# One planned list for attention and the feed-forward layers: the pairs m = 8 to 13 move into the second half of the first two chunks

## The chip, the cores and the metric

The kernel runs on one core of one Trainium2 chip. The metric is device time in microseconds (us). The core's engines are TensorE (PE in the profile; PEld is its weight loading), VectorE (DVE), ScalarE (ACT), GpSimd (POOL) and SyncE (SP). SP, ACT and POOL also issue DMAs. Each engine works through its own list of instructions in order; semaphores tie the lists together.

## What is computed

Banded attention of 8 batches, 8 heads, 576 positions and 64 features, and on its output a two-layer feed-forward network with a leaky ReLU. Cut to what matters:

```python
batch, n_heads, seq, head_dim = (8, 8, 576, 64)
n_tokens, d_model, d_ff = (4608, 512, 2048)
...
scores = scale * np.matmul(q, k.transpose(0, 1, 3, 2))
mask = (rel >= 0) & (rel < window)          # window = 64
scores = np.where(mask, scores, -1000000000.0)
scores = scores - np.max(scores, axis=-1, keepdims=True)
attn = np.exp(scores)
attn = attn / (np.sum(attn, axis=-1, keepdims=True) + 1e-09)
attn_out = np.matmul(attn, v)
...
x = attn_out.transpose(0, 2, 1, 3).reshape(B * S, H * D)
h = x @ w_in
g = np.maximum(0.01 * h, h)
return (g @ w_out)
```

## The kernel before, in words

**Tiling.** The 4608 tokens are 9 chunks of 512 (`CH`). A block of 64 queries of one batch is a unit; there are 72 units (`NU`), eight to a chunk, and attention handles them in pairs, m = 0 to 35, four pairs to a chunk. The hidden width of 2048 is 16 slices f of 128 (`FT`; `half` is 8). Numbers are kept as a high and a low part (`F32R` tiles; hi and lo, wh and wl, gh and gl), and each product is three matmuls: high by high, high by low, low by high.

**Weights.** They arrive as 64-bit floats, 32 tiles n (`fetch_w`, L200, through three buffers `raw`). Each passes `bits` (L215), `sign` (L219), `abs` (L223, on ACT), `clamp` (L227), `join` (L232), `chi` (L235, on ACT) and `rest` (L241). Even n are slices of w_in, odd n of w_out.

**The feed-forward layers.** Chunks 0 to 2 go by jobs (c, f): `mm1` (12 matmuls, L508), then on ACT the leaky ReLU and the high part, on DVE the low part, then `mm2` (12 matmuls, L554) one job later. Chunks 3 to 8 go in three product stages of two chunks each (`s` = 0, 1, 2): the first layer as 7 block products instead of 8 for each of 8 slices (L1103, 336 matmuls), the second as plain matmuls (L1128, 384). These stages read prepared weights from HBM (`w_first`, `w_second`) through a ring of four tiles that POOL fills (L1090).

**Who sets the order.** Up to the 19 jobs of `JOBS` the order is written out by hand in `ORDER`, before its bar. Then a loop over 16 jobs (chunks 0 and 1, f = 8 to 15; L641 to L674) weaves five steps of `late`, the part of `ORDER` after the bar, into each job (`PACE`), and from the sixth job on the attention of m = 8 to 11 (`scores_2`, `shield_2`, `second_2`, `sums_2`, `values_2`, `invert_2`, `norm_2`). From the eighth job on it also spreads over the jobs the 40 stores of weights to HBM (`kept`, L632: 24 to `w_first`, 16 to `w_second`). Everything after that loop is entered into a plan with `op`: an engine, an estimated duration, what it comes after, a rank. `arrange` then simulates five engines, always takes the ready operation of the lowest rank, and so writes each engine's list. A load counts 0.08 us on SP and about 2.2 us until it lands; the matmuls of attention count as ready 0.5 us after their inputs.

**One pair m in the plan** (`attend`, `normalise`): `scores_of` (PE, L268, into the PSUM banks s and t); `shield_of` (DVE, L781: scale and mask into an SBUF tile, two halves j); `all_of` with max (POOL, L787, a reduction over the partitions whose result stands on all of them); `minus_of` (DVE, L791); `exp_of` (ACT, L795). For m < 20 (`early`) the sums are matmuls with ones (`add_of`, L808) copied out by ACT (`sums_of`, L815); for later m they are two more reductions on POOL. Then `compact_of` or `compact_early` (SP DMA, L822, L819) brings the sums to a 128 x 8 tile, `inverse_of` (DVE, L826, L827) inverts it, `rows_of` (SP, L830) stores it to HBM, `spread_of` (SP, two DMAs, L840) reads it back spread over partitions, `values_of` (PE, L849) multiplies by v, `take_of` (ACT, L856, early only) copies that out of PSUM, `product_of` (DVE, L860) scales it, `keep_of` (SP, two DMAs with runs of 64 numbers, L864) stores it to `x_rows`. There are two buffers of each kind, taken by m % 2.

m = 8 to 11 take no such trip: POOL's sums stand on all partitions (L440), the reciprocal is taken there 512 wide (L467), and `norm_2` writes chunk 2's x tiles directly.

**Between attention and products.** `x_build` reads x_rows back (SP, L928), forms the sums of blocks the seven products need (DVE, L936) and splits them (ACT L952, DVE L955). `prepared` does the same for w_in: fetch from `w_single` (ACT queue, L1042), joins (DVE, L1045), high (ACT, L1048), low (DVE, L1051), four stores to `w_first` (ACT queue, L1055). Both have to wait for buffers that chunk 2's jobs (`early_first`, L977; `early_second`, L984; leaky ReLU L1005, high L1008, low L1011) set free.

Of the kernel before, what the change touches and what calls it, by code (L numbers as in the profile page):

```python
# [24 lines left out]
P = 128  # L25
# [12 lines left out]
PAIRED = 12  # L38
PACE = 5
KEPT = 7  # L40
# [56 lines left out]
def band_attention_ffn(ctx: ExitStack, tc: tile.TileContext, qT, kB, vW, vL, w_in, w_out, eye_mask, out, outT):  # L97
# [43 lines left out]
    def k_of(m):  # L141
        if m >= PAIRED:
            return (ks[0], later.get("k"), ks[1])[(m - PAIRED) % 3]
# [42 lines left out]
    w_first = dram.tile([half * 7 // 4, P, 4, 512], F32, name="w_first")  # L186
    w_second = dram.tile([half, P, 2, 1024], F32, name="w_second")

    def first_at(f, k):
        n = 7 * f + k  # L190
        return w_first[n // 4, :, n % 4].rearrange("p (i c) -> p i c", i=2)
# [203 lines left out]
    def scores_2(u):  # L395
        if u >= NU:
            return
        ps = [bank(next(t), f"s{u}_{j}") for j, t in enumerate((of_a, of_h))]
        quarter_scores(u // 2, ps, False)
        probs[u] = ps  # L400
        load_k(u // 2 + 1)
        load_q(u // 2 + 2)

    def shield_2(u):

        if u >= NU:
            return
        ps = probs.pop(u)
        a = mask_of(u).bitcast(F32)
        n = a.shape[1]  # L410
        a = flat(a)[:, None, :].broadcast_to([P, H // n, n * QB])
        for j in range(2):
            e, s = (x.rearrange("a (b c) -> a b c", c=n * QB) for x in (probs_of[:, j], ps[j]))
            nc.vector.scalar_tensor_tensor(e, s, SCALE, a, ALU.mult, ALU.add)
            if j == 0:
                first_most = most(u, j)
        exps_2(0, first_most)
        probs[u] = most(u, 1)

    def most(u, j):  # L420
        mx = temps[:, 512:]
        nc.gpsimd.partition_all_reduce(mx, probs_of[:, j], P, ReduceOp.max)
        return mx

    def exps_2(j, mx):
        e = probs_of[:, j]
        nc.vector.tensor_tensor(e, e, mx, ALU.subtract)
        nc.scalar.activation(e, e, AF.Exp)

    def second_2(u):  # L430

        if u < NU:
            exps_2(1, probs.pop(u))

    def sums_2(u):
        if u >= NU:
            return
        raw = flat(wk.tile([P, 512, 2], U32, tag="raw", bufs=3, name=f"n{u}")).bitcast(F32)
        for j in range(2):
            nc.gpsimd.partition_all_reduce(raw[:, 512 * j : 512 * j + 512], probs_of[:, j], P, ReduceOp.add)  # L440
        probs[u] = raw

    def values_2(u):
        if u >= NU:
            return
        raw = probs.pop(u)
        v = [v_heads(u // 2, w) for w in range(2)]
        ps = bank(next(of_a), f"o{u}")
        for w in range(2):
            for p in range(NP):  # L450
                for j in range(2):
                    c = (2 * p + w) * QB
                    nc.tensor.matmul(
                        ps[64 * j : 64 * j + 64, c : c + QB], v[w][:, 2 * p + j, :D], probs_of[:, j, c : c + QB],
                        start=True, stop=True,
                    )
        probs[u, 0] = ps, raw
        load_v(u // 2 + 1)

    def invert_2(u):  # L460
        if u >= NU:
            return
        ps, raw = probs[u, 0]
        r, t = raw[:, :512], raw[:, 512:]
        nc.vector.tensor_scalar_add(r[:64], r[:64], 1e-9)
        nc.vector.tensor_scalar_add(r[64:], t[64:], 1e-9)
        nc.vector.reciprocal(r, r)  # L467

    def norm_2(u):
        if u >= NU:  # L470
            return
        ps, raw = probs.pop((u, 0))
        r, t = raw[:, :512], raw[:, 512:]
        nc.vector.tensor_tensor(t, ps, r, ALU.mult)
        hi, lo = x_of(u)
        t = t.rearrange("a (b c) -> a b c", b=NP)
        nc.scalar.copy(hi, t)
        return partial(nc.vector.tensor_tensor, lo, t, hi.bitcast(F32), ALU.subtract)

    later = {}

    def open_room():

        e, n, v = (wk.tile([P, 512, 2], U32, tag="raw", bufs=3, name=f"late_{x}") for x in "env")
        e, n, v = (flat(x).bitcast(F32).rearrange("p (a b) -> p a b", a=2) for x in (e, n, v))
        k = flat(wk.tile([P, NP, 2, D], F32, tag="y", bufs=1, name="late_k").rearrange("p a b c -> p a (b c)"))
        o = [wk.tile([P, 512], F32, tag="o", name=f"late_o{i}") for i in range(2)]
        later.update(e=e, n=n, v=v, k=k.rearrange("p (a b c) -> p a b c", a=UNITS, b=NP))  # L490
        later["o"] = o, (temps[:, :512], temps[:, 512:])

    def e_of(m):
        return (probs_of, later["e"])[m % 2]
# [33 lines left out]
    def reload(c):  # L528

        ts = {}  # L530
        for i in (0, 2)[: 1 + c]:
            raw = flat(wk.tile([P, 512, 2], U32, tag="raw", bufs=3, name=f"s{c}_{i}")).bitcast(F32)
            ts[i], ts[i + 1] = raw[:, :DM], raw[:, DM:]
        for i, t in ts.items():
            nc.sync.dma_start(t, sums[c, i])
            sums[c, i] = t

# [22 lines left out]
    def evict(c, i, f, split):  # L560
        ps = acc.pop((c, i))
        t0 = c * CH + i * P
        if f < FT - 1:
            o = probs_of[:, i % 2]
            nc.scalar.copy(o, ps)
            sums[c, i] = dram.tile([P, DM], F32, name=f"sum{c}_{i}")
            nc.sync.dma_start(sums[c, i], o)
            return
        if split:
            o = sums.pop((c, i))  # L570
            nc.vector.tensor_tensor(o, ps, o, ALU.add)
        else:
            if c == NCHUNK - 1 and i >= 2:
                o = flat(wk.tile([P, 512, 2], U32, tag="raw", bufs=3, name=f"o{c}_{i}")).bitcast(F32)[:, :DM]
            else:
                o = wk.tile([P, DM], F32, tag="o", name=f"o{c}_{i}")
            if c == NCHUNK - 1 and i % 2 == 0:
                nc.vector.tensor_copy(o, ps)
            else:
                nc.scalar.copy(o, ps)  # L580
        nc.sync.dma_start(out[t0 : t0 + P, :], o)

    def flush():
        while due:
            due.pop(0)()

    whole, first, second = slice(0, CH), slice(0, CH // 2), slice(CH // 2, CH)
    def weave(others, mine):

        both = [((k + 0.5) / len(x), i, f) for i, x in enumerate((others, mine)) for k, f in enumerate(x)]  # L590
        for _, _, f in sorted(both, key=lambda x: x[:2]):
            f()


# [30 lines left out]
    order, late = ([step(x) for x in part.split()] for part in ORDER.split("|"))  # L625
    for f in order:
        f()
    prev = jobs[-1]
    jobs = [(c, half + k, whole) for c in range(2) for k in range(half)]

    def store(to, f, *at):
        nc.sync.dma_start(to, both[f][at])  # L632

    kept = []
    for f in range(half):
        for x, a, k in ((f, 0, 0), (f, 256, 4), (f + half, 256, 5)):
            kept.append(partial(store, first_at(f, k), x, slice(None), slice(2), slice(a, a + 256)))
    for f in range(FT):
        kept.append(partial(store, w_second[f // 2, :, f % 2].rearrange("p (i c) -> p i c", i=2), f, slice(None), slice(2, 4)))
    first_late = len(jobs) - UPC - 3  # L640
    for n, job in enumerate(jobs):  # L641
        weave(mm1(*job), late[n * PACE : (n + 1) * PACE])
        if first_late <= n < len(jobs) - 1:
            u = TURNED - 2 + (n - first_late) // 2 * 2
            ahead = u + 2 < UNITS * PAIRED
            if (n - first_late) % 2 == 0:
                if u >= TURNED:
                    values_2(u)
                if ahead:
                    scores_2(u + 2)  # L650
                    shield_2(u + 2)
            else:
                if ahead:
                    second_2(u + 2)
                low = norm_2(u) if u >= TURNED else None
        mm2(*prev)
        flush()
        if first_late < n < len(jobs) - 1:
            if (n - first_late) % 2 == 0:
                invert_2(u)  # L660
            else:
                if low:
                    low()
                if ahead:
                    sums_2(u + 2)
        if n == 4:
            reload(0)
        if n == 14:
            reload(1)
# [603 lines left out]
```

## Time and profile before

| | us |
|---|---|
| median of 3 runs (lowest, highest) | 973.12 (970.44, 976.64) |
| profiled execution, device time | 973.42 |
| its span, first to last instruction | 971.7 |
| PE busy in the span | 904.4 (93%) |
| PEld, DVE, ACT, POOL busy | 724.8, 537.9, 332.7, 312.5 |
| second halves of chunks 0 and 1 | from 128.22 |
| chunk 2 | from 225.52 |
| first product stage, s = 0 | from 399.27 |
| s = 1 and s = 2 | from 636.62 to the end |

How to read what follows: a windows row gives a stretch of the span, its length, the busy time of each engine in it with the number of instructions, the granted TensorE clock (1.00 is full), the mean busy share of the 16 DMA engines and what they moved. A timeline row gives start, duration, engine, line, operation, output <- input and count; in brackets the idle time before it and what ended it. A waits row gives who waited for whom: us in total, times, longest. A lines row gives a group's busy time and the mean ns of one.

### The profile page before, as it was taken

The numbers are of one execution on the slowest core, as the hardware profiler recorded it, in microseconds if no ns is written. First come the engines' busy times: TensorE is split into PE (matmuls) and PEld (weight loads), VectorE is DVE, ScalarE is ACT, GpSimd is POOL, SyncE is SP. The second block draws the span as 40 slices with busy tenths as digits, with TensorE's granted clock in tenths as the row PEclk, the third lists the DMA queues.
The fourth block names the chain that finished last, engine by engine and source line by source line (L and its number), as shares of the span: only waits on it lengthen the run. The fifth ranks groups of instructions, "written<-read, shape, count | busy, mean of one in ns | idle before, by whom it ended". The sixth has DMA issues, their size and how long they took to land. (4 is left out here: it accounts for less than half of the span.)

```text
span 971.7 us, 17011 instructions
## 1 busy us (share of the span) xinstructions
PE 904.4 (93%) x6938; PEld 724.8 (75%) x6938; DVE 537.9 (55%) x847; ACT 332.7 (34%) x565; POOL 312.5 (32%) x206
## 2 busy tenths in 40 slices
PE   9999999999978876699888988989999999999998
PEld 6878888888756654577676777878888888888886
DVE  7999854883656467654455877333335513333221
ACT  5666543332423323222222323123334313333221
POOL 5330002850333217577565756400100101010010
PEclk9999999999999888799899989999999999999999
DMA  9766632699587987678686978665558756655562
GB/s 329 244 218 216 200 109 76 210 344 383 165 234 214 286 261 231 200 224 258 184 252 185 303 191 267 177 225 200 190 188 275 235 202 227 198 193 186 204 219 84
DMA packets 126686, 213.46 MB, mean 220 GB/s; under 512 B 64272, under 2 KB 78736, under 8 KB 115088
## 3 DMA queue, kind: packets, MB, share of 16 engines
q0 software_dynamic: 12960, 94.38, 29.1%
q1 hardware_dynamic: 84960, 62.44, 21.3%
q10 hardware_dynamic: 28688, 55.55, 18.0%
q8 instruction: 55, 0.90, 0.4%
q14 instruction: 23, 0.19, 0.1%
HBM read 167.58 MB, written 44.66 MB: 218 GB/s over the span
## 5 line engine op out<-in xcount | busy, mean ns | idle before, releaser
L1103 PE MATMUL m<-pfew,p 128*128 128x512 f32 x720 | 173.2, 396 | 1.8 <-DVE pxa L1112 1.8
L1103 PEld LDWEIGHTS m<-pfew,p 128*128 128x128 f32 x720 | 136.4, 191 | 31.3 <-DVE pxa L1112 2.2
L1128 PE MATMUL y<-gs,p 128*128 128x512 f32 x576 | 140.1, 396 | 0.4 <-ACT p L1131 0.4
L1128 PE MATMUL y<-pxa,p 128*128 128x512 f32 x576 | 140.5, 400 | 0.0
L1128 PEld LDWEIGHTS y<-pxa,p 128*128 128x128 f32 x576 | 110.8, 193 | 24.4
L1128 PEld LDWEIGHTS y<-gs,p 128*128 128x128 f32 x576 | 107.4, 187 | 26.6 <-ACT p L1131 0.8
L787 POOL PARTITION_ALL_REDUCE late_o<-e x40 | 96.0, 2415 | 90.7 <-DVE e L781 36.8
L787 POOL PARTITION_ALL_REDUCE g<-late_e x40 | 97.5, 2454 | 41.0 <-DVE late_e L781 15.6
L1090 POOL DMA_DIRECT2D p<-w_second x48 | 25.6, 534 | 181.2 <-PE y L1128 136.7
L1115 ACT ACTIVATE p<-p 128x512 f32<-128x512 f32 x63 | 39.7, 631 | 127.8 <-DVE p L1112 127.8
L1090 POOL DMA_DIRECT2D p<-w_first x42 | 22.5, 537 | 180.5 <-PE m L1103 115.0
L1103 PE MATMUL m<-pxb,p 128*128 128x512 f32 x288 | 74.2, 406 | 2.5 <-DVE p L1131 2.5
L1112 DVE TENSOR_TENSOR p<-m,pxa 128x512 f32<-128x512 f32 x63 | 43.4, 690 | 54.5 <-PE m L1103 53.6
L1112 DVE TENSOR_TENSOR pxa<-m,pxa 128x512 f32<-128x512 f32 x57 | 39.3, 689 | 60.0 <-PE m L1103 54.7
L1103 PEld LDWEIGHTS m<-pxb,p 128*128 128x128 f32 x288 | 56.2, 197 | 15.1 <-DVE p L1131 2.9
L1121 DVE TENSOR_TENSOR gs<-p,gs 128x512 fp32r<-128x512 f32 x48 | 38.2, 796 | 50.3 <-ACT gs L1118 50.2
L554 PE MATMUL acc<-p,gs 128*128 128x512 f32 x264 | 64.8, 395 | 0.0
L268 PE MATMUL s<-q,k 64*64 64x64 f32 x1648 | 43.6, 239 | 18.7 <-DVE late_e L781 10.7
L268 PEld LDWEIGHTS s<-q,k 64*64 64x64 f32 x1648 | 37.4, 151 | 28.5 <-issue 11.9
L554 PEld LDWEIGHTS acc<-p,gs 128*128 128x128 f32 x264 | 49.0, 188 | 10.7
L1121 DVE TENSOR_TENSOR pxa<-p,pxa 128x512 fp32r<-128x512 f32 x36 | 29.5, 818 | 43.4 <-ACT pxa L1118 43.4
L1118 ACT CAST gs<-p 128x512 fp32r<-128x512 f32 x48 | 29.6, 619 | 68.5 <-PE y L1128 68.4
(146 smaller groups left out, 1335.5 us busy)
## 6 DMA issues: line engine op xcount, KB each, us to landing
p<-w_second POOLq DMA_DIRECT2D x48, 1024.0 KB, 5.3
p<-w_first POOLq DMA_DIRECT2D x42, 1024.0 KB, 5.1
w_first<-p ACTq DMA_DIRECT2D x32, 256.0 KB, 3.9
raw<-w_out ACTq DMA_DIRECT2D x15, 512.0 KB, 3.9
raw<-w_in ACTq DMA_DIRECT2D x14, 512.0 KB, 3.6
x_rows<-late_n SPq DMA_DIRECT2D x48, 128.0 KB, 5.0
p<-x_rows SPq DMA_DIRECT2D x24, 256.0 KB, 5.3
outT<-p SPq DMA_DIRECT2D x24, 256.0 KB, 3.7
```

Of the source, the lines that this page charges most:

```text
L268: nc.tensor.matmul(ps[j][t, c : c + QB], k[i][s, p], q[s, w, p], start=not begun and (not more or (w, p) == (0, 0)), stop=not begun and no ...
L554: nc.tensor.matmul(acc[c, i], a[:, ts], b, start=begin and n == 0, stop=end and n == 2)
L787: nc.gpsimd.partition_all_reduce(sum_of(m, j), e_of(m)[:, j], P, what)
L1090: nc.gpsimd.dma_start(ring[n], of.rearrange("p a b -> p (a b)"))
L1103: nc.tensor.matmul(tiles[b], w[:, 256 * i + 128 * kt : 256 * i + 128 * kt + 128], x[j][:, 512 * kt : 512 * kt + 512], start=begin and c == ...
L1112: nc.vector.tensor_tensor(to(), tiles[b], x(), ALU.add)
L1115: nc.scalar.activation(to(), to() if b is None else tiles[b], AF.Prelu, alpha=0.01)
L1118: nc.scalar.copy(g_pair(q)[0], x())
L1121: nc.vector.tensor_tensor(g_pair(q)[1], x(), g_pair(q)[0].bitcast(F32), ALU.subtract)
L1128: nc.tensor.matmul(tiles[i], a, b, start=f == 0 and k == 0, stop=f == FT - 1 and k == 2)
```

## The change

From the end of the hand-written part of `ORDER` on, all work is entered into the plan. The loop over the 16 jobs is gone, with `weave`, `PACE`, `KEPT`, `reload`, `flush` and the seven functions `scores_2` to `norm_2`.

* The rest of the weights' conversion is entered step by step, each after the step before it and its buffers, with rank 0.2 or 0.3. The 40 stores are entered with rank 2.0 after the steps that make their tiles.
* `walk` is the 16 jobs of chunks 0 and 1 and the 16 of chunk 2 in one loop; each `mm1` is entered as two halves, and `second_step` comes two jobs behind instead of one.
* All pairs m = 8 to 35 go through `attend` and `normalise`, m = 8 to 13 entered in that loop, m = 14 to 35 after `prepared`. The sums of all of them are reductions on POOL (`add_of` now). m = 8 to 11 write chunk 2's x tiles with `high_early` and `low_early` in place of `keep_of`. Chunk 2's first job waits for them (`x2`). Every shield also comes after `gate`, which follows the last weights' steps and the eviction of the first jobs' sums.
* Buffers: three tiles of probabilities by m % 3; maxima and sums each have one tile per half j; one tile for the spread rows; v has one buffer from m = 8 on; k and q keep two.
* `keep_of` is one DMA of 2 KB per partition, and `x_build` reads 2 KB rows. `w_first` is laid out by partition, so that a ring fill and the stores of `prepared` have longer runs; those stores are two per slice instead of four.
* Sums of chunks 0 and 1 are read back into xa1 and xb (`reload_of`) instead of the raw buffers.
* The planner's figures: a load 0.5 us of SP and 4.0 us to land, a bulk load 0.45 and 6.0, matmuls of attention ready 2.0 us after their inputs, 4.0 us for m >= 20 (`LAG`), with 0.5 added to the rank of everything of m >= 20. DVE operations with two SBUF inputs count 1.05 instead of 0.95.

The diff, cut to its core:

```diff
-PAIRED = 12
-PACE = 5
-KEPT = 7
+PAIRED = 8
+EARLY = 20
+FIRST_LATE = 14
+LAG = 2.0
...
     def v_of(m):
         if m >= PAIRED:
-            return (vs[0], later.get("v"))[m % 2][:, :, : H * D]
+            return vs[0][:, :, : H * D]
...
     def e_of(m):
-        return (probs_of, later["e"])[m % 2]
+        return probs_of if m % 3 == 0 else later["ef"[m % 3 - 1]]
...
+        o[kind] = op(engine, us, step(name), *(o.get(b) for b in before), *more, rank=0.3)
+    all_in = [weights_of[n][k] for n in (28, 29, 30, 31) for k in ("join", "rest")] + [weights_of[27]["rest"]]
...
+                stores[x].append(load(fn, *ready[x], rank=2.0))
...
     def keep_of(m):
-        for w in range(UNITS):
-            nc.sync.dma_start(
-                x_rows[m, :, 256 * w : 256 * w + 256].rearrange("p (k c) -> p k c", k=NP),
-                n_of(m).rearrange("p (k w c) -> p k w c", w=UNITS, k=NP)[:, :, w],
-            )
+        nc.sync.dma_start(x_rows[m], done_of(m))
...
+            o["v"] = bulk(partial(load_v, m, nc.scalar), before["X1"])
...
+            "PE", 1.0, partial(scores_of, m), o.get("q"), o.get("k"), before.get("E1"), before.get("E0"), three.get("take"), *takes, s_free,
+            before.get("S"), rank=0.5 + late, lag=LAG if early(m) else 2 * LAG,
...
+            o[f"E{j}"] = op("DVE", ONE, partial(shield_of, m, j), o["S"], three.get("V"), three.get(f"A{j}"), gate, before.get("E1"), rank=0.8 + late)
...
+            o[f"A{j}"] = op("POOL", 3.5, partial(add_of, m, j), o[f"X{j}"], before.get(f"c{j}"), rank=0.4 + late)
+            o[f"c{j}"] = load(partial(compact_of, m, j), o[f"A{j}"], two.get("rows"), rank=0.3 + late)
...
+        spread = [load(partial(spread_of, m, j), o["rows"], before.get("Y"), rank=0.3 + late) for j in range(2)]
...
+        if m < UPC // UNITS * LEAD:
+            hi = op("ACT", ACTS, partial(high_early, m), o["Y"], *x2_free, rank=0.8 + late)
+            o["kept"] = [op("DVE", TWO, partial(low_early, m), hi, rank=0.8 + late)]
+            x2.extend(o["kept"])
         else:
...
+            o["kept"] = [load(partial(keep_of, m), o["Y"], rank=0.35 + late)]
...
+    walk = [(c, half + k) for c in range(2) for k in range(half)] + [(2, f) for f in turn_of]
...
+    for n, (c, f) in enumerate(walk):
+        next_main(6 * MM, partial(early_first, n, 0), lows.get(n - 2), *ready[f], *(x2 if c == 2 else ()))
+        first = next_main(6 * MM, partial(early_first, n, 1))
+        if n == 0:
+            next_main(12 * MM, lambda: mm2(*prev))
...
+            gate = op("SP", 0.02, open_room, *all_in, s_free)
+        if n > 1:
+            second_step(n - 2)
...
+        if n == half + 1:
+            x2_free = evicted[0]
+            for m in range(PAIRED, FIRST_LATE):
+                attend(m, gate)
+                if m > PAIRED + 1:
+                    normalise(m - 2)
...
+        hurry = 0.4 + 0.15 * f
+        freed = slot_free[14 + f % 2] if f < 2 else prepared[f - 2]
+        got = [bulk(partial(fetch, i), *freed, *all_in, rank=hurry + 0.1) for i in range(2)]
...
+    for m in range(FIRST_LATE, NU // 2 + 2):
+        if m == EARLY:
+            normalise(m - 2)
             normalise(m - 1)
         if m < NU // 2:
-            attend(m, opened)
-        if m > PAIRED and not last:
-            normalise(m - 1)
+            attend(m, None)
+        if m not in (EARLY, EARLY + 1):
+            normalise(m - 2)
```

More of the change, by code (lines that the diff above doesn't have):

```diff
@@ L638, in band_attention_ffn @@
[L638 to L669, printed above, removed]
-        if n >= KEPT:
-            for f in kept[(n - KEPT) * len(kept) // (len(jobs) - KEPT) : (n - KEPT + 1) * len(kept) // (len(jobs) - KEPT)]:
-                f()
-        prev = job
```

561 lines of the change are left out of this document (238 added, 323 removed).

## The prediction

> **What bounds the kernel now.** The page came first: its span, and TensorE's two rows over 40 slices.
>
> ```profile
> span 971.7 us, 17011 instructions
> PE   9999999999978876699888988989999999999998
> PEclk9999999999999888799899989999999999999999
> ```
>
> TensorE is full for the first quarter and for the last third. It is not in the slices between, and there its granted clock falls too. The kernel's stages put bounds on those slices: the second halves of the jobs of chunks 0 and 1 begin at 128.22, chunk 2 at 225.52, the first of three product stages at 399.27, the second at 636.62. The windows view with these bounds (columns: stretch, its length, busy time of PE, PEld, DVE, ACT, POOL with counts, clock, DMA share, GB/s):
>
> ```profile
> 128.22:161.00 32.78, 32.78 (x204) 26.91 (x203) 13.30 (x24) 13.14 (x23) 0.00 (x0) 1.00 0.37 118
> 161.00:225.52 64.52, 64.52 (x567) 53.01 (x566) 47.63 (x49) 20.49 (x34) 40.98 (x16) 1.00 0.74 254
> 225.52:399.27 173.75, 137.45 (x1614) 105.26 (x1612) 101.28 (x164) 52.87 (x91) 56.40 (x30) 0.90 0.80 247
> 399.27:636.62 237.35, 213.33 (x1875) 169.74 (x1873) 143.48 (x200) 68.82 (x116) 153.73 (x84) 0.95 0.75 225
> 636.62:971.70 335.08, 331.12 (x1440) 271.28 (x1440) 118.76 (x181) 100.59 (x164) 29.55 (x56) 0.99 0.60 201
> ```
>
> Chunk 2's stage idles TensorE 173.75 - 137.45 = 36.3 us, the first product stage 24.0, all others together some 7. So I price those two stages, from what they need. The timeline of PE has the pieces:
>
> ```profile
> 128.22 2.88 PE L508 MATMUL h<-pxa,p 128*128 128x512 f32 x12
> ...
> 133.69 2.88 PE L508 MATMUL h<-pxa,p 128*128 128x512 f32 x12
> ...
> 158.37 1.16 PE L268 MATMUL s<-q,k 64*64 64x64 f32 x64
> ...
> 252.86 0.64 PE L808 MATMUL sum<-e,p 128*32 128x256 f32 x8
> 253.42 1.15 PE L849 MATMUL o<-e,v 128*64 128x64 f32 x32
> ```
>
> A job is 133.69 - 128.22 = 5.47 us. A pair of attention blocks (one m) takes 1.16 for its scores, 0.64 for its sums, 1.15 for its values. Chunk 2's stage needs 16 x 5.47 + 8 x 2.95 + two scores = 113.4 us, so 60 us of its 173.75 are lost: 36 idle, 24 to the lower clock behind the idling. A later product stage takes 335.08 / 2 = 167.5; the first also has 14 scores and 16 values, 34.6, so 202 are needed and 35 lost. Some 95 us can be won in all. Who holds TensorE, from the waits of PE in 225:400 and in 399:640:
>
> ```profile
> PE s L268 <- DVE late_e L781: 8.4, 2, 7.6
> PE acc L984 <- ACT gs L1008: 7.2, 2, 6.6
> PE s L268 <- ACT late_n L856: 7.1, 4, 6.5
> ...
> PE s L268 <- DVE e L781: 9.0, 5, 2.9
> PE s L268 <- DVE late_e L781: 5.6, 4, 2.3
> PE o L849 <- ACT e L795: 4.6, 3, 2.2
> ```
>
> All of these are waits of an ordered list. TensorE stands at an attention step whose input is late, with the products queued behind it.
>
> **The attention's pace.** The timeline of POOL shows when each m's maxima begin:
>
> ```profile
> 161.84 1.78 POOL L422 PARTITION_ALL_REDUCE g<-e  x1 [84.68 <-DVE e L414]
> ...
> 200.68 1.78 POOL L422 PARTITION_ALL_REDUCE g<-e  x1 [0.85 <-DVE e L414]
> ...
> 241.27 3.55 POOL L787 PARTITION_ALL_REDUCE late_o<-e  x2 [28.05 <-DVE e L781]
> ...
> 317.48 3.76 POOL L787 PARTITION_ALL_REDUCE g<-late_e  x2 [4.55 <-DMA c<-g]
> ...
> 387.09 3.62 POOL L787 PARTITION_ALL_REDUCE late_o<-e  x2
> ...
> 450.43 1.86 POOL L787 PARTITION_ALL_REDUCE late_o<-e  x1
> ```
>
> m = 8 to 11 run from 161.84 to 200.68, 12.95 us each. POOL then has no attention for the 28 us before m = 12. From there to m = 19 it is (317.48 - 241.27) / 7 = 10.9 each, with sums on TensorE; from m = 22 to 26, 63.3 / 4 = 15.8, with sums on POOL. And m = 19, the last that the product stage needs, has its maximum at 317.48, while the products begin at 399.27: a tail of 82 us.
>
> **The change, part by part.** (1) *Earlier start.* The tail of the weights' conversion, five steps per job before, is now placed by readiness. Its last tile before:
>
> ```profile
> 148.18 0.33 ACTq L200 DMA_DIRECT2D raw<-w_out  x1
> ...
> 151.69 0.43 DVE L215 TENSOR_SCALAR raw<-raw 128x512 uint32<-128x512 uint32 x1 [2.17 <-DMA raw<-w_out]
> ...
> 160.37 0.68 DVE L241 TENSOR_TENSOR p<-w,p 128x512 fp32r<-128x512 f32 x1
> ```
>
> The load lands in 3.5 us and the steps take 9.4, all of it spread to fit the jobs. Only the buffer of tile 28 holds that load back; I put its issue at 135 instead of 148.18 (estimate), and so the weights' end, which now gates every shield, at 148, and the first maximum at 150. The bounds are 145 and 161.84, as now. No pause follows m = 11: that is where most of the lead comes from.
>
> (2) *Sums on POOL for m = 12 to 19.* TensorE loses 8 x 0.64 = 5 us. POOL gains 16 sums:
>
> ```profile
> L440 POOL PARTITION_ALL_REDUCE n<-e x8 | 26.2, 3271 | 5.1 <-ACT e L428 5.1
> ```
>
> 16 x 3.27 = 52 us, hidden while POOL stays under its pace: 2 x 1.78 + 2 x 3.27 = 10.1 us an m. Without that cover 10.1 would be the floor of the pace. The sums also lengthen each m's chain by 6.5.
>
> (3) *m = 8 to 11* exchange the 512-wide reciprocals for three small DMA trips (sums to a compact tile, inverses to HBM, rows back), each with SP and DVE waiting in order. Pace for all twelve: from 10.9 to 15.8 by the rows above. I take 12.95, which has the same four POOL operations, beside the same jobs. Maximum of m = 19: 150 + 11 x 12.95 = 292.5.
>
> (4) *The tail from there.* Floor: m = 12 went from 241.27 to its kept rows at 266.6, which land in 5.0, 30.3 in all; plus 6.5 for the POOL sums and 5.3 for the reading back; its DVE and ACT steps come on top. That is 42.
>
> ```profile
> 265.58 0.99 SPq L864 DMA_DIRECT2D x_rows<-late_n  x2
> ...
> x_rows<-late_n SPq DMA_DIRECT2D x48, 128.0 KB, 5.0
> p<-x_rows SPq DMA_DIRECT2D x24, 256.0 KB, 5.3
> ```
>
> Ceiling: the 82 of now. The planner now counts 4.0 us for a load's landing and 0.5 for its issue (2.2 and 0.08 before), close to these rows, so its lists should wait less; but the same prep and x_build work shares DVE, ACT and SP. I take 66, nearer the measured end. Start of the products: 358.5. TensorE could not be there before 128.2 + 32 x 5.47 + 12 x 2.31 + two scores = 333, so 25 us of waits remain in the sum. Chunk 2's own start waits for m = 11: 150 + 39 + 36 = 225, when TensorE gets there too; some us late would vanish in those 25.
>
> (5) *Margins of the lists.* Scores and values are now placed 2 us after readiness, for the late m's 4 us, instead of 0.5. In the first product stage each of the twelve attention waits is at most 2.9, and they sum to 19.2 of the 24.0 idle. 3.5 us more margin would take all of them if nothing else came later; I leave 15 of the 35 lost, as there is now one buffer each for the values' input, the sums and the spread rows. Bounds: 8 and 35. What waits anew: POOL's sums for the compact DMA of the m before (POOL's next maximum and the ring's fills stand behind), TensorE's values for a 512 KB load (the products stand behind).
>
> (6) *Rows of 2 KB, w_first by partition, sums reloaded to other tiles, second layers two jobs behind.* Costed at nothing: fewer packets on a queue that takes 21.3% of the engines' time,
>
> ```profile
> q1 hardware_dynamic: 84960, 62.44, 21.3%
> ```
>
> and the rest moves the same bytes. If x_rows' traffic lost its cover it would be part of the tail.
>
> **Sum**, against the profiled execution's 973.42 (median of the runs 973.12, so it is taken as it is): 358.5 + (202 + 15) + 335.1 + 1.7 around the span = 912.
>
> **A rule against it.** These rows (lines view; DVE's timeline) show a subtract beside POOL's work and one mostly without it, and a DVE operation issued 0.4 us behind a sum on POOL:
>
> ```profile
> L791 DVE TENSOR_TENSOR e<-e,late_o 128x512 f32<-128x512 f32 x24 | 26.5, 1103 | 0.9 <-POOL late_o L787 0.9
> ...
> L427 DVE TENSOR_TENSOR e<-e,g 128x512 f32<-128x512 f32 x8 | 5.5, 685 | 5.3 <-POOL g L422 5.3
> ...
> 166.20 3.31 POOL L440 PARTITION_ALL_REDUCE n<-e  x1
> ...
> 166.61 2.46 DVE L522 TENSOR_TENSOR gs<-g,gs 128x512 fp32r<-128x512 f32 x1 [2.26 <-ACT gs L518]
> ```
>
> The Trainium skill, SBUF — State Buffer, Who interferes with whom, says that a DVE instruction with two SBUF inputs and a GpSimd one that reads SBUF take turns on a shared port, the later blocking fully. The trace agrees: that operation took 2.46 us, where its neighbours take 0.69. What it would make of the time is the second rival below.
>
> **Rivals.** *TensorE-bound.* The tail falls to its floor and the products start at 333: 333 + 202 + 8 + 336.8 = 880, without any loss 872. For it: 150 + 11 x 10.9 + 42 = 312 is below 333. Against: DVE is busy 101 us already in chunk 2's stage, and would be so in 108.
>
> *DVE held by POOL.* Prep has 5 operations with two SBUF inputs for each of 8 tiles, x_build 28, the products 8: 76, each up to 1.103 - 0.685 = 0.42 longer, 32 us. With 101.3 that is 133, and for an in-order engine at 90% 148: the products start at 225.5 + 148 = 373. If the first product stage then gains nothing (237.35): 947.
>
> *Nothing gained.* The waits only move: 963 to 983.
>
> *Slower: the stores ahead of the small trips.* In SP's list the 40 stores of weights are ready at once and SP is idle, so most go out together from 128, where before they lay between 173 and 231:
>
> ```profile
> 173.57 0.94 SPq L632 DMA_DIRECT2D w_first<-pfew  x2
> ...
> 221.87 9.46 SPq L632 DMA_DIRECT2D w_second<-p  x9
> ```
>
> At 1.05 us each they fill 40 us of SP. They compete with the last raw tiles, and m = 8's compact DMA stands behind them; DVE stands at its reciprocal with the jobs' low parts behind. The first maximum is then at 163, the pace 15.8, the tail 82: 419 + 237.35 + 336.8 = 993. It decides once the products start after 409. Against it: DMA is only 0.37 busy in 128 to 161, and m = 8 needs its trip only at 160.
>
> **Chances.** Forecast 0.45, TensorE-bound 0.15, DVE held 0.20, nothing 0.07, slower 0.13. Faster by over 1% (about what a measurement of this kernel can tell from no change): 0.79; within 1%: 0.08; slower: 0.13. Range: 872, TensorE's floor, to 980, which is first maximum 150, pace 15.8, tail 82 (406) and an unchanged product stage.
>
> **What would show it.** First maximum on POOL near 150 and no pause until m = 19's near 292; chunk 2's first matmul near 226; the products' near 358 (now 399.27), their second stage 217 later. Wrong if the pace is over 16, if DVE waits for a compact DMA in 150 to 180, if DVE is over 90% busy from 226 on, or if TensorE still waits for shields in the first product stage.

## The result, and the profile after

The changed kernel takes 908.15 us (median of 4 runs, 907.11 to 909.0); the kernel before, beside it on the same chip, 973.33 (4 runs, 970.44 to 976.64). The ratio is 0.9329, with a 95% interval of 0.9297 to 0.936: 65 us are gone, where 61 were forecast. The profiled execution took 907.11 us. Medians here are over all runs, while the ratios leave out the runs that fell in a slower state (one of e3's ten, four of the kernel before's below). Line numbers are those of the changed kernel from here on; L855 and L864 are chunk 2's two layers and the second halves of chunks 0 and 1 (`early_first`, `early_second`), L659 and L662 POOL's maxima and sums, L717 the scaling by the spread rows, L1006 the first layer of the product stages.

The page of the changed kernel: its span, TensorE's busy tenths and its clock in 40 slices, the packets, and SP's queue.

```profile
span 905.3 us, 16930 instructions
PE   8999999789999998999999999999999999999998
PEclk9999999989999999999999999999999999999999
DMA packets 82557, 214.49 MB, mean 237 GB/s; under 512 B 16048, under 2 KB 26416, under 8 KB 70960
q1 hardware_dynamic: 41120, 58.51, 19.5%
```

The valley from slice 12 to 27 is filled but for an 8 in the sixteenth, and the clock no longer falls there. One notch stays, in the eighth slice (158 to 181 us), with a lower clock in the ninth behind it. The stages as windows (columns as before):

```profile
129.06:149.59 20.53, 20.53 (x150) 16.80 (x149) 13.77 (x26) 10.25 (x20) 0.00 (x0) 1.00 0.92 313
149.59:229.00 79.41, 71.51 (x762) 57.00 (x761) 49.13 (x56) 23.57 (x42) 57.55 (x24) 0.96 0.58 205
229.00:357.50 128.50, 122.94 (x1090) 98.18 (x1088) 86.32 (x127) 45.50 (x76) 67.06 (x29) 0.99 0.72 236
357.54:557.47 199.93, 196.83 (x1840) 157.69 (x1840) 136.17 (x194) 68.60 (x114) 133.96 (x77) 0.99 0.83 271
557.47:905.30 347.83, 341.76 (x1793) 278.44 (x1791) 143.60 (x214) 105.09 (x173) 71.39 (x73) 0.99 0.65 214
```

TensorE idles 7.9 us in the attention's first stretch, 5.6 in the second, 3.1 in the first product stage. Beside the rows before, one thing isn't a gain: some attention now runs into the second product stage. The last values stand there,

```profile
557.47 1.52 PE L1006 MATMUL m<-pxb,p 128*128 128x512 f32 x6
...
627.67 1.15 PE L706 MATMUL o<-late_f,v 128*64 128x64 f32 x32
```

so the last row carries 3 scores and 5 values, 9.2 us, where the kernel before has none. The first product stage now has 12 scores and 11 values instead of 11 and 14, 2.3 us less. All waits of TensorE that the view lists between 128 and 900 fit in four lines:

```profile
PE h L855 <- DVE gs L875: 10.0, 2, 7.9
PE m L1006 <- DVE pxa L1015: 5.1, 3, 2.0
PE m L1006 <- ACT p L887: 2.5, 1, 2.5
PE m L1006 <- DVE pxb L832: 1.0, 1, 1.0
```

None of them is an attention step any more; before, most were. The pace of the attention on POOL, and the pause in it (in brackets: idle time, and what ended it):

```profile
149.59 3.55 POOL L659 PARTITION_ALL_REDUCE g<-late_f  x2 [71.96 <-DVE late_f L650]
...
158.60 3.31 POOL L662 PARTITION_ALL_REDUCE late_o<-late_f  x1
176.16 3.23 POOL L662 PARTITION_ALL_REDUCE late_o<-e  x1 [14.24 <-DMA compact<-late_o]
...
302.00 3.64 POOL L659 PARTITION_ALL_REDUCE g<-late_e  x2 [0.32 <-DVE late_e L650]
```

The first maximum is at 149.59, m = 19's at 302.00. At 176.16 POOL has stood for 14.24 us behind a compact DMA. The queue of SP and DVE's timeline say why:

```profile
140.18 5.49 SPq L623 DMA_DIRECT2D w_first<-p  x6
...
156.30 9.92 SPq L623 DMA_DIRECT2D w_second<-p  x7
...
169.42 10.46 SPq L673 DMA_DIRECT2D compact<-late_o  x3
```

```profile
176.22 2.20 DVE L677 TENSOR_SCALAR compact<-compact 128x8 f32<-128x8 f32 x1 [9.14 <-DMA compact<-late_o]
```

The 40 stores of weights go out between 134 and 169 in one pile, and m = 8's sums, which POOL ends at 156.9 and 161.9, are fetched only from 169.42 on. DVE stands 9.14 us for them, with the low part of a job's g (L875) behind, and TensorE 7.9 us for that. That is the mechanism of the slower rival, at the place that it named. It just costs less there. Chunk 2, too, starts later than before (225.52) for it:

```profile
239.30 1.54 PE L855 MATMUL h<-pxa,p 128*128 128x512 f32 x6
```

Of the 13.8 us, 7.9 are this wait, 0.8 a later start of the stretch, and 4.9 attention that has moved ahead of chunk 2 (14.2 us of scores and values instead of 9.3).

### The profile page after: what moved, and what is told of

The parts are those of the page before. It is cut to its first block, busy times and chain, and to the rows that moved or that the text cites. A ratio compares the mean times of both kernels' runs of the same rounds, so it can differ in the third digit from the quotient of the medians.

```text
span 905.3 us, 16930 instructions
## 1 busy us (share of the span) xinstructions
PE 879.0 (97%) x6874; PEld 706.9 (78%) x6874; DVE 540.2 (60%) x843; ACT 329.5 (36%) x560; POOL 362.6 (40%) x222
## 4 chain that ended last, share of the span: by engine, by line
PE 80%; DMA 9%; DVE 7%; issue 2%; ACT 1%; POOL 1%; ACTq 0%; SPq 0%; DVEq 0%; POOLq 0%
PE y L1031 29%; PE m L1006 24%; PE h L855 6%; PE acc L864 5%; PE h L418 4%; PE acc L454 4%; PE s L266 3%; PE o L706 3%; DMA late_r<-rows 2%; DMA compact<-late_o 1%; DMA rows<-compact 1%; DMA x_rows<-late_n 1%; DVE p L946 1%; DMA raw<-w_in 1%; DVE late_n L717 1%
## 5 line engine op out<-in xcount | busy, mean ns | idle before, releaser
L1006 PE MATMUL m<-pfew,p 128*128 128x512 f32 x720 | 172.2, 393 | 5.1 <-DVE pxa L1015 5.1
L1006 PEld LDWEIGHTS m<-pfew,p 128*128 128x128 f32 x720 | 134.4, 188 | 34.5 <-DVE pxa L1015 6.0
L1031 PE MATMUL y<-pxa,p 128*128 128x512 f32 x576 | 136.5, 391 | 0.0
L1031 PEld LDWEIGHTS y<-pxa,p 128*128 128x128 f32 x576 | 107.7, 188 | 23.4
L864 PE MATMUL acc<-p,gs 128*128 128x512 f32 x324 | 80.3, 396 | 0.0
L1006 PE MATMUL m<-pxb,p 128*128 128x512 f32 x288 | 73.3, 399 | 3.5 <-ACT p L887 2.5
L659 POOL PARTITION_ALL_REDUCE g<-late_f x20 | 36.5, 1853 | 98.8 <-DVE late_f L650 98.7
L662 POOL PARTITION_ALL_REDUCE late_o<-late_f x20 | 65.1, 3272 | 24.1 <-ACT late_f L670 14.4
L864 PEld LDWEIGHTS acc<-p,gs 128*128 128x128 f32 x324 | 59.9, 188 | 13.3
L662 POOL PARTITION_ALL_REDUCE late_o<-e x18 | 59.2, 3308 | 20.0 <-DMA compact<-late_o 14.2
L1006 PEld LDWEIGHTS m<-pxb,p 128*128 128x128 f32 x288 | 54.4, 192 | 16.0 <-ACT p L887 2.6
L662 POOL PARTITION_ALL_REDUCE late_o<-late_e x18 | 59.6, 3326 | 12.3 <-ACT late_e L670 6.0
L855 PE MATMUL h<-pxa,p 128*128 128x512 f32 x228 | 57.1, 399 | 2.1 <-DVE gs L875 2.1
```

The lines of the kernel that those rows point to most:

```text
L659: nc.gpsimd.partition_all_reduce(most_of(j), e_of(m)[:, j], P, ReduceOp.max)
L662: nc.gpsimd.partition_all_reduce(sum_of(j), e_of(m)[:, j], P, ReduceOp.add)
L855: nc.tensor.matmul(ps, a[:, k, :], b[:, k], start=i == 0, stop=i == len(terms) - 1)
L864: nc.tensor.matmul(acc[c, i], a[:, i * P : (i + 1) * P], b, start=begin and k == 0, stop=n in ends and k == 2)
L1006: nc.tensor.matmul(tiles[b], w[:, 256 * i + 128 * kt : 256 * i + 128 * kt + 128], x_part(OF_X[k], j, kt), start=begin and c == 0, stop=c = ...
L1031: nc.tensor.matmul(tiles[i], a, b, start=f == 0 and k == 0, stop=f == FT - 1 and k == 2)
```

## The experiments

Twelve kernels ran. All ratios are against the kernel before, timed on the same chip; its medians there were 971.22 (first batch: e1, e2, e4, e6), 971.03 (second: e3, e5, e7, e8) and 973.32 (third: e9 to e12). A difference in us between two kernels is that of their medians; where the ratios, each to the kernel before of its own batch, make another of it (times 972), that stands beside it. "Products" is the start of the first product stage. "The change" is the changed kernel. The theory was the prediction's own: an earlier start without a pause gives the lead, and the margins of the lists take the product stage's waits. The rivals were the planner's transfer figures as the cause, and the stores as a cost still inside the result.

**e1_pause** puts the pause back: m = 14 may not begin before chunk 2's fourth job.

```diff
+        if m == FIRST_LATE:
+            at[m]["S"]["after"].append(firsts[19])
```

> The changed kernel, but the scores of m = 14 also come after the 20th job's first layer (the fourth of chunk 2), so attention pauses again, some 30 us, where the changed kernel has m = 14's maximum at 231. Theory (the gain is the lead: no pause, an earlier start): the last early pair is 30 us later and the products with it, about 388 instead of 357.5, and the time is 930 to 940 against 908. Rival (the planner's better figures and margins bring the gain, the lead is slack): at most 915.

It took 926.03 us (925.19 to 928.35), ratio 0.9549 [0.9512, 0.9587], 18 us more than the change (21 by the ratios), below both ends of the theory's range but nearer to it than to the rival's. The timelines of its POOL and of its PE:

```profile
258.85 3.55 POOL L659 PARTITION_ALL_REDUCE g<-late_f  x2 [26.57 <-DVE late_f L650]
```

```profile
383.34 2.83 PE L1009 MATMUL m<-pxb,p 128*128 128x512 f32 x6
```

POOL idles 26.57 us, m = 14 comes 27.6 later than the change's 231.29, and the products 25.8 later. So in the sum the lead runs through to the products. It doesn't do so step by step: m = 19 is 35.1 us later,

```profile
337.11 3.59 POOL L659 PARTITION_ALL_REDUCE g<-late_e  x2
```

and the tail behind it is 46.2 us instead of 55.5. Of the 26 us, 5 to 8 come back before the end; where stays open.

**e4_stores** spreads the 40 stores, three to a job from the fourth job on.

```diff
+    stored = sorted((x for f in stores for x in stores[f]), key=lambda x: x["n"])
+    for i, x in enumerate(stored):
+        x["after"].append(firsts[3 + i // 3])
```

> The changed kernel with the 40 weight stores spread, three behind each job from the fourth on, instead of all at once. Theory (the stores stand ahead of m = 8's small DMAs on SP, cost POOL 14.2 us and TensorE 7.9, and this runs through to the products): POOL's pause at 162 to 176 and TensorE's at 175 to 183 vanish, the products start 8 to 12 us earlier, 896 to 901. Rival (a later wait takes the place, as the tail has slack): the two pauses vanish and the time stays at 905 to 909.

897.93 us (895.12 to 903.7, 6 runs), ratio 0.926 [0.9222, 0.9297]: the fastest kernel of the study, 10 us below the change (7 by the ratios, whose intervals just touch). Its page, SP's queue, POOL and PE:

```profile
PE   9999999999999998999999999999999999999998
```

```profile
156.60 0.54 SPq L673 DMA_DIRECT2D compact<-late_o  x1
```

```profile
149.24 3.55 POOL L659 PARTITION_ALL_REDUCE g<-late_f  x2 [71.91 <-DVE late_f L650]
...
291.87 3.63 POOL L659 PARTITION_ALL_REDUCE g<-late_e  x2 [0.32 <-DVE late_e L650]
```

```profile
347.58 1.91 PE L1010 MATMUL m<-pxb,p 128*128 128x512 f32 x5 [1.01 <-DVE pxb L832]
```

The notch is gone, m = 8's compact DMA goes out at 156.60 instead of 169.42, and m = 19 comes at 291.87. That is (291.87 - 149.24) / 11 = 12.97 us an m, the pace that was forecast (12.95); the changed kernel's is (302.00 - 149.59) / 11 = 13.86. The products start 10.0 us earlier, and the profiled execution's span is 10.9 shorter (894.4).

**e12_gate** is e4 with the first shields held until the sixth job; it asks what the early start alone is worth.

```diff
+    gate["after"].append(firsts[5])
```

> The changed kernel with the stores spread, and the gate of all shields also after the sixth job's first layer, so that the first maximum comes at about 162 as before the change, 12 us later. Theory (the start runs through to the products one for one): 908 to 911 against 898. Rival (attention has slack before the products): 898 to 902.

905.9 us (903.63 to 908.5, 6 runs), ratio 0.9344 [0.9293, 0.9395]: 8.0 us above e4, for a first maximum that is 8.5 us later,

```profile
157.72 3.55 POOL L659 PARTITION_ALL_REDUCE g<-late_f  x2 [79.44 <-DVE late_f L650]
```

with the products 7.9 us later. The gate moved the start by 8.5 us instead of the expected 12, so neither expected range applies as it stands; 8.0 for 8.5 fits the theory. Again it isn't so at each step: m = 19 (297.33) is only 5.5 us later, and the tail 2.4 longer.

**e2_margin** takes the margins away: scores and values count as ready 0.5 us after their inputs again.

```diff
-            before.get("S"), rank=0.5 + late, lag=LAG if early(m) else 2 * LAG,
+            before.get("S"), rank=0.5 + late, lag=0.5,
...
-    ... o["X0"], o["X1"], *free, before.get("V"), rank=0.5 + late, lag=LAG if early(m) else 2 * LAG)
+    ... o["X0"], o["X1"], *free, before.get("V"), rank=0.5 + late, lag=0.5)
```

> The changed kernel with the old margin of 0.5 us for scores and values of all pairs, instead of 2 and 4. Theory (the wider margins took the waits of the first product stage): TensorE waits for shields and exponentials again in that stage, 10 to 20 us with the lower clock behind them, 918 to 928. Rival (those waits went because the inputs come earlier, the margin does nothing): 905 to 911.

901.75 us (900.87 to 903.6), ratio 0.9298 [0.9261, 0.9334]. The intervals of this and the change overlap, so it can't be called better, but it certainly isn't slower. Products at 355.26, the second stage 204.1 behind. The theory of the margins falls here, though not because nothing moved: the first product stage now holds 15 scores and 13 values, 5.9 us more attention than in the change, and is 4.2 us longer.

**e3_loads** keeps the margins and gives the planner its old figures for transfers (without the old term for the bytes on the wire).

```diff
-    def load(fn, *after, rank=1.0, us=0.5, land=4.0):
+    def load(fn, *after, rank=1.0, us=0.08, land=2.2):
...
-        return op("ACT", 0.45, fn, *after, rank=rank, lag=1.5, land=6.0)
+        return op("ACT", 0.1, fn, *after, rank=rank, lag=1.5, land=4.1)
```

> The changed kernel with the planner's old figures for transfers: a load 0.08 us of SP and 2.2 to land, a bulk load 0.1 of ACT and 4.1. Theory (the truer figures shortened the tail and the waits in the lists): the tail from m = 19's maximum to the products grows from 55 towards the 82 of before, 918 to 935. Rival (buffers and the lead carry the gain, lists are not that sensitive): 903 to 912.

965.96 us (958.39 to 974.25, 10 runs), ratio 0.9929 [0.9885, 0.9973]. Four numbers, which no instruction carries, take back 58 of the 65 us, far more than either side expected. Its PE timeline, and waits of ACT and of DVE:

```profile
157.56 2.60 PE L266 MATMUL s<-q,k 64*64 64x64 f32 x64 [18.14 <-ACT e L463]
```

```profile
ACT e L463 <- DMA sum<-e: 20.1, 1, 20.1
...
DVE late_n L717 <- DMA late_r<-rows: 91.1, 19, 9.0
```

There are two places. Early, ACT copies the first jobs' sums to the tile that their store reads (L463), the list believes the store to be quick, and it stands 20.1 us behind the pile of weight stores. Later, DVE stands 91.1 us at the spread rows, 19 times. In the changed kernel this second row is

```profile
DVE late_n L717 <- DMA late_r<-rows: 19.3, 7, 4.2
```

Such a total alone proves little, though: e4, the fastest kernel, has

```profile
DVE late_n L717 <- DMA late_r<-rows: 42.8, 17, 5.3
```

What counts is what stands behind the wait, and in which stage, as the next run shows.

**e11_loads_spread** takes the first of the two places out: the old figures on e4, with its spread stores.

> The changed kernel with the stores spread and the planner's old figures for transfers. With all stores at once the old figures cost 58 us, 18 of them where TensorE's first scores stood behind the sums' DMAs in the stores' queue. Theory (that pile is one part, the other is DVE and SP standing in order at trips that the list takes for shorter than they are): 925 to 940, and DVE still waits over 60 us for the spread rows. Rival (the pile is all of it): 898 to 905.

950.97 us (947.49 to 955.22), ratio 0.9809 [0.9745, 0.9873], 53 us above e4. Its PE timeline, the waits of DVE between 128 and 640 and between 359 and 592, those of PE between 128 and 640, and the first product stage as a window, at last the same window in e4:

```profile
359.27 1.66 PE L1010 MATMUL m<-pxb,p 128*128 128x512 f32 x6
...
591.29 1.65 PE L1010 MATMUL m<-pxb,p 128*128 128x512 f32 x6 [1.27 <-DVE p L1038]
```

```profile
DVE late_n L717 <- DMA late_r<-rows: 84.5, 18, 11.7
```

```profile
DVE late_n L717 <- DMA late_r<-rows: 46.7, 9, 11.7
```

```profile
PE m L1010 <- DVE pxa L1019: 16.5, 7, 4.9
```

```profile
359.27:591.29 232.02, 207.33 (x1943) 162.88 (x1936) 133.94 (x200) 68.35 (x115) 137.89 (x78) 0.96 0.74 245
```

```profile
347.58:546.41 198.83, 196.72 (x1839) 157.64 (x1840) 136.22 (x194) 68.56 (x114) 133.89 (x77) 0.99 0.84 273
```

The products start 11.7 us later than in e4. But most of it goes in the product stage: 232.0 us against 198.8, of which TensorE idles 24.7 us against 2.1. Work moved in and the lower clock account for 10.6 (207.33 - 196.72), yet the rest behind it is not shorter for that but 10.6 longer. DVE stands 46.7 us at the spread rows in this stage (12.3 in e4's) with the adds (L1019) and low parts (L1028) of the products behind, and TensorE waits for those: at 577.50 DVE goes on after 11.68 us at the rows, the low part follows at 579.31, and TensorE goes on at 580.05 after a wait of 5.16. The kernel before, 237.35 us with 24.0 idle, shows the same one step on, with a shield (L781) behind the spread rows (L860) and TensorE's scores behind the shield:

```profile
505.20 0.69 DVE L860 TENSOR_TENSOR late_n<-o,late_n 128x512 f32<-128x512 f32 x1 [5.91 <-DMA late_n<-rows]
...
506.41 0.68 DVE L781 SCALAR_TENSOR_TENSOR e<-s,away 128x512 f32<-128x512 f32 x1
```

```profile
507.24 0.33 PE L268 MATMUL s<-q,k 64*64 64x64 f32 x1 [2.81 <-DVE e L781]
```

In that stage its DVE stood 33.5 us at spread rows in all (the first row of this view of 128 to 640; all eight waits lie behind 399):

```profile
DVE late_n L860 <- DMA late_n<-rows: 33.5, 8, 8.8
```

**e6_before_figures** asks whether the figures do it alone: the kernel before with the new figures and margins in its planner, nothing else. In this order a part of its attention is computed from other values, presumably since steps that share a buffer come in another sequence; instructions, shapes and transfers are the same, so its time is weak evidence.

```diff
-        return op("SP", 0.08, fn, *after, rank=rank, us_more=kb)
+        return op("SP", 0.5, fn, *after, rank=rank, us_more=kb)
...
-                x["end"] = max(wire, t) + 2.2
+                x["end"] = max(wire, t) + 4.0
```

> The kernel before with only the planner's figures of the change: loads 0.5 us of SP and 4.0 to land, bulk loads 0.45 and 6.0, DVE operations with two SBUF inputs 1.05, margins of 2 us for the early and 4 us for the late scores, sums and values. Attention keeps its place and pause. Theory (the lead is most of the gain): the products start 15 to 30 us earlier, the first product stage gains some 15, 930 to 950. Rival (the figures are the gain): 905 to 920.

955.0 us (946.77 to 959.51), ratio 0.9841 [0.9776, 0.9906], 16 us below the kernel before, above both expected ranges. Products at 392.49 instead of 399.27, the first product stage 224.3 instead of 237.35. So the figures and margins are worth some 16 us (9 to 22 by the interval) without the new structure, and the new structure with the old transfer figures 5 to 7 (e3) or, with spread stores, 19 to 22 (e11). Together they give 65, with spread stores 72 to 73. Neither half explains the change alone.

**e8_rank** takes the 0.5 off the rank of the attention of m >= 20.

```diff
-        o, late = at.setdefault(m, {}), 0.0 if early(m) else 0.5
+        o, late = at.setdefault(m, {}), 0.0
```

> The changed kernel without the 0.5 added to the ranks of all work of m >= 20, so that late attention goes ahead of the products' work as it did before. Theory (the first product stage gained by the late pairs giving way, as the margins did not do it): that stage takes 10 to 25 us longer with waits on shields and exponentials, 912 to 925. Rival (the stage gained because its pairs have three buffers and start earlier): 903 to 911.

916.01 us (915.07 to 917.09), ratio 0.9438 [0.9378, 0.9498], 8 us more (11 by the ratios). Products at 355.48, the second stage at 567.18: the stage takes 211.7 instead of 199.9. Of the 11.8 us, 4.6 are attention that moved into the stage (13 scores and 14 values instead of 12 and 11); TensorE's idle time there grows from 3.1 to 8.6. The expected waits on shields and exponentials aren't there; TensorE stands at the products' adds and low parts. So the rank is a second thing that keeps the product stage short, by some 7 us. It ranks the late attention's steps, those on DVE among them, behind the products' adds.

**e5_rows** stores and reads x_rows with two DMAs of 256-byte runs again.

```diff
-        nc.sync.dma_start(x_rows[m], done_of(m))
+        for w in range(UNITS):
+            nc.sync.dma_start(turned_rows(m)[:, :, w], by_unit(done_of(m))[:, :, w])
```

> The changed kernel with attention rows in HBM in runs of 64 numbers (256 bytes) again, written and read back in two DMAs each. Theory (forecast: costed at nothing beside the rest): 906 to 913. Rival (the 2 KB rows are a main part of the gain, the SP queue had 41 thousand packets more): 918 to 930.

913.5 us (911.4 to 919.01, 6 runs), ratio 0.9417 [0.9371, 0.9462], with

```profile
DMA packets 126334, 214.50 MB, mean 236 GB/s; under 512 B 65969, under 2 KB 76337, under 8 KB 114737
```

The intervals of the two ratios don't overlap: the 2 KB rows are worth some 5 us by the medians (9 by the ratios), for 43,800 packets less, and one store and one read less per m. Which of the two it is, packets or issues, isn't shown.

**e7_onejob** brings the second layer back to one job behind the first.

```diff
-        if n > 1:
-            second_step(n - 2)
+        if n > 0:
+            second_step(n - 1)
```

> The changed kernel with the second layers of chunks 0 to 2 one job behind the first again instead of two. Theory (forecast: costed at nothing): 906 to 913. Rival (the second job of distance keeps late high and low parts off TensorE): TensorE waits for the low parts before the second layers, 915 to 930.

903.93 us (901.16 to 906.26), ratio 0.9309 [0.9255, 0.9362], no difference from the change.

**e9_both** (e4 and e2 together) and **e10_three** (these and e7) ask whether small gains add up.

> The changed kernel with the stores spread and the old margin of 0.5 us. If the two gains of 10 and 6 us come from different places they add: 890 to 894. If the narrow margin only won back what the stores had cost (TensorE at the attention steps while m = 8 was held), nothing is added: 896 to 899.

> As the one with spread stores and the old margin, with the second layers one job behind the first as well. Additive: 886 to 891. Rival (with less slack in the lists TensorE waits for low parts): 893 to 900.

They don't. e9 took 902.14 us (899.77 to 907.32, 6 runs), ratio 0.9311 [0.9261, 0.936]; e10 909.93 (903.6 to 913.67, 6 runs), ratio 0.938 [0.9327, 0.9434]. e9 has not gained on e4, and e10 is slower than e4, though each edit by itself was at or below the change. So an edit that shifts the lists is worth several us either way by the shift alone, which is argued from these two totals and not traced step by step. The effects of e4 and e8 are no larger than that; e4's has POOL's closed pause behind it as well, e8's the idle time. e4 is the version to keep.

## Why the prediction was right, and where it was wrong

Sign and size came out, and so did two of the stage times, though only in part for the reasons given. The products start at 357.54 (358.5 forecast), and from there to the end it took 547.8 us (217 + 335.1 = 552.1).

**What bounds the kernel: two counts were off.** By the matmul counts of the two windows, chunk 2's stage before has 13 scores and 10 values, not 10 and 8, and the first product stage 11 and 14, not 14 and 16. So chunk 2's stage needed about 119 us and lost about 54, not 60, with less for the clock than 24; the product stage needed 196 and lost 41, not 35. The total of some 95 stays.

**Step 1, the start and the missing pause: right.** The last raw load went out at 132.97 (135 forecast), the last step of the weights ended at 148.82 (148), and the first maximum came at 149.59 (150). e12 and e1 show that in the sum both the start and the pause run through to the products, 7.9 us for 8.5 and 25.8 for 27.6. Chunk 2's first matmul, forecast near 226, came at 239.30: the forecast had no wait before it and no attention moved ahead of it.

**Step 2, sums on POOL: right.** POOL's reductions of m = 8 to 19 never bound the pace. With the pile gone it is 12.97, above the 10.1 that POOL needs.

**Steps 3 and 4, pace and tail: two errors that cancelled.** m = 19 was 9.5 us later than forecast (302.0 for 292.5), by POOL's 14.24 us behind the stores. The tail was 10.5 shorter (357.54 - 302.00 = 55.5 for 66). That the products start within 1 us of the forecast is luck. The reason given for a short tail, that the planner's transfer figures lie nearer the rows, isn't shown. With the old figures and no pile (e11) the products come 11.7 us later than in e4, but m = 19 is 6.6 later already:

```profile
298.46 3.62 POOL L659 PARTITION_ALL_REDUCE g<-late_e  x2 [0.85 <-DVE late_e L650]
```

Its tail is 60.8 us for e4's 55.7. With the new figures tails of 61.7 (e2) and 46.2 (e1) occur too. What took the rest of the 82 stays open. In the choice between floor 42 and ceiling 82, 66 leaned too far to the old end.

**Step 5, the margins: the step that failed.** The prediction credited the 2 and 4 us of margin with 20 of the first product stage's 35 lost us. The stage did lose that much less; over both stages some 10 us remain ((199.9 - 202) + (347.8 - 335.1) = 10.6). But without the margins the kernel is no slower (e2), and with them the stage still takes 232.0 us when the transfer figures are the old ones (e11). What removes the waits are the transfer figures (232.0 against 198.8, e11) and, for some 7 us, the lower rank of the late attention (e8). The prediction took the list of TensorE for the place, since TensorE's waits named attention steps there. The place was one engine further back, as the rows under e11 show for both kernels: DVE stood in order at spread rows which the planner expected 2.2 us after their issue, and which land in 5.1 there and in 4.4 in the changed kernel (DMA issues of both):

```profile
late_n<-rows SPq DMA_DIRECT2D x32, 128.0 KB, 5.1
```

```profile
late_r<-rows SPq DMA_DIRECT2D x56, 128.0 KB, 4.4
```

The prediction did see the figures, but weighed them in step 4 only.

**Step 6: not quite nothing.** The second layers' two jobs cost nothing (e7), the rows gain 5 to 9 us (e5).

**The rivals.** *Slower, by the stores ahead of the small trips*: its mechanism happened, and cost 7 to 10 us (e4), not 81. What was said against it, that m = 8 needs its trip only at 160, gave false comfort, since the pile lasted until 169. It stayed small, as far as the rows show, because only one m met the pile: in e4, without it, the pace of the later m and the tail (55.7) are much the same. *DVE held by POOL*: DVE was busy 86.32 of the 128.5 us from 229 on, 67%, and not over 90%. Waiting beside POOL is there to be seen, as the last section shows, but not as a wait of TensorE. *TensorE-bound*: not reached; e4, with 219.4 us from 128.2 to the products and 5.6 of them idle, comes nearest. Without these 5.6 its products would start at about 342, so the floor of 333 was some 9 us too low. *Nothing gained*: excluded, though e3 shows that four figures of the planner stand between it and the result.

**The signs named beforehand.** For the forecast spoke the first maximum, the products' start, a pace of 13.86 (not over 16), DVE's 67%, and that no shield is among TensorE's waits in the first product stage. One sign of being wrong came true, DVE's wait for a compact DMA before 176. The attention did pause, for the 14.24 us of POOL, and chunk 2 came at 239.30. The second product stage came 199.9 us after the first, not 217, in part because attention ran on behind it.

## What to carry to other kernels

When a list is planned, the durations that the planner assumes are part of the kernel: compare each of them with the trace's own rows (issue, landing) before any structure is changed, for here they decided 53 to 58 us that no instruction shows. Where an in-order engine waits, ask which engine's list put the instruction there; TensorE's wait for an add was DVE's wait for a load. Work without a due time, such as the weight stores, should be given one, or it goes out as a pile exactly when the first small transfer of the next phase needs the queue.

## What the runs showed of the hardware

The same store took SP longer where the DMA engines were full. In the pile, where the window from 156.30 to 166.22 has a DMA share of 1.03, seven issues of `w_second<-p` took 9.92 us, 1.4 us each (the row above); in e4 three took 1.73, 0.6 each, at 216.88 with a share of 0.78, and three 4.02, 1.3 each, at 222.31 with a share of 1.04. One store alone took 0.32 at 238.55 with a share of 1.04, so the share isn't all of it; no run varies it alone.

Small DVE operations, too, can be held beside a reduction on POOL. The addition of 1e-9 to the 128 x 8 sums (L677, a tensor_scalar) took 2.20 us at 176.22, beside the POOL sum that begins at 176.16, and 0.16 at 191.04, just behind a maximum that begins at 191.02, so not each such neighbour holds it; a subtract issued 0.13 us behind a sum took 2.74, where eight subtracts of the kernel before, mostly without that neighbour, took 0.685 on average:

```profile
191.04 0.16 DVE L677 TENSOR_SCALAR compact<-compact 128x8 f32<-128x8 f32 x1
```

```profile
158.73 2.74 DVE L666 TENSOR_TENSOR e<-e,g 128x512 f32<-128x512 f32 x1 [1.04 <-POOL g L659]
```

On average it stays mild: 18 subtracts of one kind took 1.329 us each,

```profile
L666 DVE TENSOR_TENSOR late_e<-late_e,g 128x512 f32<-128x512 f32 x18 | 23.9, 1329 | 3.5 <-POOL g L659 3.5
```

and DVE as a whole lay at 67% before the products. The Trainium skill (SBUF — State Buffer, Who interferes with whom) counts tensor_scalar, in its two-port modes, among the operations that can contend with GpSimd for the shared port pair; the 2.20 for 0.16 agrees.
